# Exchanged weight halves by eight SP transfers instead of two GpSimd copies, and one warming product fewer

## The chip, the core and the metric

The kernel runs on one core of a Trainium2 chip. TensorE (PE) multiplies, VectorE (DVE), ScalarE (ACT) and GpSimd (POOL) work elementwise, and SyncE (SP) issues DMA transfers, as ACT and GpSimd can too. The metric is device time in microseconds; the time before is the median of 3 runs.

## The reference

A softmax over 7 taps per head (8 heads of 24 channels) weighs a causal convolution along the sequence; its result, 31232 tokens of 192 channels, goes through a multiplicative feed-forward layer:

```python
w = softmax(weight)                          # 8 x 7
out[b, s, h, g] = sum_k w[h, k] * x_pad[b, s + k, h, g]
x = out.reshape(31232, 192)
a = x @ w1                                   # 192 x 1024
b = x @ w2                                   # 192 x 1024
y = (a * b @ w3) @ w_out                     # 1024 x 1024, 1024 x 192
```

Inputs and output are float32; the kernel multiplies in bfloat16.

## The kernel before

**Work by rounds.** The tokens are cut into two halves (`NS = 2`) of 15616, and each half into rounds of `CH = 512` tokens. A round holds 512 tokens of both halves. `first_product(R)` runs over the 8 blocks of 128 features (`JT`, f = 0 to 7). For each it computes `pa` (w1) and `pb` (w2) on TensorE, ACT casts `pa` to `asb`, and VectorE multiplies `asb` by `pb` into `abT`. `second_product` multiplies `abT` by `W_sb`, the product of w3 and w_out made once on the chip near the start, and stores the output. Between the blocks of the first rounds, other steps are hung in by hand (`between`): convolutions, transposes, the products for `W_sb`.

**Why there are exchanged halves.** The 192 channels are cut into three parts of `Q = 64` (k = 0, 1, 2). An operand tile has 128 partitions: the 64 channels of one part for token half r = 0 in partitions 0 to 63, and for r = 1 in partitions 64 to 127. A product of L599 uses only the 64 partitions of its half, so the weights of each part have to stand in both partition halves. `wn[0]` holds w1's first 128 channels, `wn[1]` those of w2, `wn[2]` the remaining 64 of w1 (partitions 0 to 63) and of w2 (64 to 127). `wsw[k]`, in the profile `ws`, holds `wn[k]` with the two partition halves exchanged. `w_of` chooses between the two. For `pb` of each block the second and third product read `wsw[1]`: first its partitions 64 to 127, then 0 to 63.

**Order at the start.** The order on each engine is the order of the program (a manual schedule); semaphores are set by the framework. GpSimd issues the loads of the weights in two column ranges, 0 to 384 and 384 to 1024 (L227 to L233; the last of them is `wn[1]`, L231). The exchanged halves are made by `swap_w` (L222) with copies of 64 partitions: ACT and VectorE make columns 0 to 384, VectorE 256 to 640 of `ws[0]`, GpSimd the rest in the order in which the blocks come, with transfers for x (L158) and w3 (L677) between. Columns `W2 = 768` to 1024 serve blocks 6 and 7 and are GpSimd's last copies, in the order k = 0, 2, 1:

```python
load_w3(0, 4, range(2))
for k in (0, 2, 1):
    swap_w(k, W2, DFF, P)      # P: GpSimd's copy; two halves each
load_w3(0, 4, range(2, 4))
```

Meanwhile TensorE runs warming products on zeros (`warm`, L241) whose results nobody reads: 6 and 3, then 2, then 4 of 256 columns (L297) right after the product `bps` from which VectorE casts `Aband`, the band matrix of the convolution. Then come the first convolution (L331), its transposes (L419) and `first_product(0)`. SP has three loads at the start and its next instruction is the store of `convo` at 29.22 us.

Of the kernel before, what the change touches and what calls it, by code (L numbers as in the profile page):

```python
# [16 lines left out]
def kernel(  # L17
# [10 lines left out]
    nc = tc.nc  # L28
# [4 lines left out]
    DFF = moe_w1.shape[1]  # L33
# [10 lines left out]
    Q = 64  # L44
# [52 lines left out]
    def banks(name):  # L97
        return psum.tile([128, NS, CH], FP32, tag="banks", name=name)
# [23 lines left out]
    def group(r, e):  # L122
        return slice((2 * r + e) * C, (2 * r + e) * C + C)
# [57 lines left out]
    for r in range(NS):  # L181
        p = group(r, 0).start
# [12 lines left out]
        out=diag, in_=diag, pattern=[[-1, 128 + 8]], compare_op=ALU.is_equal,  # L195
# [13 lines left out]
    for i in range(4):  # L209
        d = diag[i * C:i * C + C, i * C + 2 * i:i * C + 2 * i + C]  # L210
        nc.vector.tensor_copy(
            out=cmask[i * C:i * C + C],
            in_=bass.AP(tensor=d.tensor, offset=d.offset, ap=[d.ap[0], [1, 2], [1, C]]))

    wn = [const.tile([128, DFF], BF16, name=f"wn{k}", tag=f"wn{k}") for k in range(3)]
    wsw = [const.tile([128, DFF], BF16, name=f"ws{k}", tag=f"ws{k}") for k in range(3)]

    W0, W1, W2 = 384, 640, 768

    def swap_w(k, lo, hi, f, halves=(1, 0)):  # L220
        for h in halves:
            f(out=wsw[k][Q * h:Q * h + Q, lo:hi], in_=wn[k][Q - Q * h:2 * Q - Q * h, lo:hi])  # L222
# [15 lines left out]
    def warm(n, wd=CH):  # L238
        t = banks("warm")
        for j in range(n):  # L240
            nc.tensor.matmul(  # L241
                t[:, j % 2, 0:wd].rearrange("p (a c) -> p a c", c=128), zeros,
                zeros.unsqueeze(1).to_broadcast([128, wd // 128, 128]), start=True, stop=True)
# [15 lines left out]
    for i in range(3):  # L259
# [3 lines left out]
        out=share[:, :, 0:K], in0=taps.unsqueeze(1).to_broadcast([H, H, K]), scalar=total,  # L263
        in1=diag[0:H, 0:H].unsqueeze(2).to_broadcast([H, H, K]), op0=ALU.mult, op1=ALU.mult)
    spread = banks("spread")
    for i in range(4):
# [6 lines left out]
        out=wsb, in_=spread[:, 0, 0:2 * H].rearrange("p (h k) -> p h k", h=H)  # L273
# [5 lines left out]
        out=cprod.rearrange("p h k (s two) -> p h k s two", two=2),  # L279
# [6 lines left out]
    p = group(1, 0).start  # L286
# [3 lines left out]
    for k in range(2):  # L290
# [3 lines left out]
            start=(k == 0), stop=(k == 1))  # L294
    nc.vector.tensor_copy(out=Aband,
                          in_=bps[:, 0, 0:C * H].rearrange("p (h s) -> p h s", s=C))
    warm(4, 256)  # L297


    xT = [const.tile([128, RING], BF16, name=f"xT{k}", tag=f"xT{k}") for k in range(NP)]  # L300
# [369 lines left out]
    def load_w3(j0, n, quarters=range(4)):  # L670
        if j0 not in w3b_of:
            t = stage.tile([128, 4 * n, GQ], BF16, tag=f"w3b{j0}", bufs=1, name="w3b")
            for j in range(j0, j0 + n, 2):
                w3b_of[j] = (t, 4 * (j - j0))
        t = w3b_of[j0][0]
        for i in quarters:
            nc.gpsimd.dma_start(  # L677
                out=t[C * i:C * i + C],
                in_=bass.AP(tensor=moe_w3.tensor, offset=j0 * 128 * DFF + i * GQ,
                            ap=[[DFF, C], [C * DFF, 4 * n], [1, GQ]]))  # L680
# [36 lines left out]
    for k in (0, 2, 1):  # L717
        swap_w(k, W1, W2, P)
    load_w3(0, 4, range(2))
    for k in (0, 2, 1):  # L720
        swap_w(k, W2, DFF, P)
    load_w3(0, 4, range(2, 4))

    trios = [tuple(range(R, R + TRIO)) for R in range(0, NR - 1, TRIO)]
# [12 lines left out]
    starts, chain, begun, room, p = {}, {}, set(), 0, -1  # L737
# [209 lines left out]
```

## Time and profile before

| | us |
|---|---|
| median of 3 runs | 511.01 (510.94 to 512.11) |
| the profiled execution | 511.07 |
| its span, first to last instruction | 509.3 |
| TensorE busy | 504.8 (99%) |
| VectorE busy | 446.6 (88%) |
| ACT busy | 347.3 (68%) |
| GpSimd busy | 229.5 (45%) |

Times in the trace are counted from the start of the span. PE stands for the products, PEld for TensorE's loads of weights, which overlap them; the ends of products are modelled. SPq is SP's queue of DMA issues, q0 the queue of GpSimd's transfers and q1 that of SP's. The bracket at the end of a row gives the engine's idle time before it and what released it. In the windows of the first 30 us the granted TensorE clock is given as 1.00 throughout; in the whole profile it is 0.999.

### The profile page before, as it was taken

To read this page: it belongs to the slowest core of one execution; us is meant where nothing else is said; L and a number is where in the kernel's file an instruction comes from. 1 tells how busy PE (TensorE), PEld (TensorE's weight loads), DVE (VectorE), ACT (ScalarE), POOL (GpSimd) and SP (SyncE) were. 2 spreads that over 40 slices of the span, in tenths; PEclk is the share of its full clock that TensorE was granted. 3 is DMA by queue.
4 is the path that set the end of the run, shared out by engine and by line. 5 is a ranking of instruction groups with operands and counts; after the bars stand their busy time and mean duration, and the time that the engine had idled before them with its cause. 6 is when DMAs were issued, how large, how long until landed. Compare 5 with 4: busy or idle time off the path is not lost.

```text
span 509.3 us, 13691 instructions
## 1 busy us (share of the span) xinstructions
PE 504.8 (99%) x5762; PEld 339.3 (67%) x5762; DVE 446.6 (88%) x403; ACT 347.3 (68%) x387; POOL 229.5 (45%) x303
## 2 busy tenths in 40 slices
PE   8999999999999999999999999999999999999997
PEld 4546865595569557855875596569557855965597
DVE  7898769999999899899989999999899999999930
ACT  6786667736778776477667767763776477457752
POOL 9965201333990597079509902970573067100000
PEclk9999999999999999999999999999999999999999
DMA  9999968999965999973979337986501500230025
GB/s 139 151 161 177 166 142 188 155 158 187 170 60 158 138 163 132 231 79 23 65 198 118 24 105 119 191 119 155 104 0 44 156 2 0 83 107 1 1 64 156
DMA packets 156825, 58.45 MB, mean 115 GB/s; under 512 B 112607, under 2 KB 156763, under 8 KB 156763
## 3 DMA queue, kind: packets, MB, share of 16 engines
q1 hardware_dynamic: 86043, 40.62, 37.2%
q0 software_dynamic: 70560, 16.85, 36.8%
q8 instruction: 45, 0.74, 0.6%
q14 instruction: 17, 0.14, 0.1%
q10 hardware_dynamic: 160, 0.10, 0.1%
HBM read 33.97 MB, written 34.85 MB: 135 GB/s over the span
## 4 chain that ended last, share of the span: by engine, by line
PE 99%; ACT 0%; DVE 0%; issue 0%
PE ops L624 32%; PE pa L599 31%; PE pb L599 31%; PE cps L331 1%; PE wps L696 1%; PE warm L241 1%; PE tps L404 0%; PE tps L419 0%; PE ops L649 0%; DVE abT L608 0%; PE cps L360 0%; ACT asb L606 0%; ACT convo L340 0%; PE bps L291 0%; ACT osb L653 0%
## 5 line engine op out<-in xcount | busy, mean ns | idle before, releaser
L608 DVE TENSOR_TENSOR abT<-asb,pb 128x1024 bf16<-128x1024 bf16 x240 | 292.7, 1221 | 30.4 <-ACT asb L606 14.5
L606 ACT CAST asb<-pa 128x1024 bf16<-128x1024 f32 x244 | 246.9, 1012 | 64.3 <-PE pa L599 64.0
L599 PEld LDWEIGHTS <-wn 64*128 64x128 bf16 x1488 | 138.6, 94 | 79.7 <-issue 1.6
L599 PEld LDWEIGHTS <-ws 64*128 64x128 bf16 x1488 | 129.7, 94 | 69.8 <-issue 1.7
L624 PE MATMUL ops<-W_sb,abT 128*128 128x192 bf16 x1936 | 163.7, 246 | 0.0
L624 PEld LDWEIGHTS <-abT 128*128 128x128 bf16 x1936 | 158.5, 98 | 6.4 <-issue 6.4
L599 PE MATMUL pb<-xT,wn 64*128 64x512 bf16 x408 | 111.2, 376 | 0.0
L599 PE MATMUL pa<-xT,wn 64*128 64x512 bf16 x408 | 110.1, 376 | 0.1
L599 PE MATMUL pa<-xT,ws 64*128 64x512 bf16 x408 | 110.2, 376 | 0.0
L599 PE MATMUL pb<-xT,ws 64*128 64x512 bf16 x408 | 108.5, 376 | 0.0
L629 ACT COPY osb<-ops 128x768 f32<-128x768 f32 (+1 forms) x61 | 48.4, 794 | 84.7 <-PE ops L624 82.9
L877 POOL COPY pace<-abT 1x2 bf16<-1x2 bf16 x57 | 10.9, 192 | 176.5 <-DVE abT L608 156.0
L599 PE MATMUL pb<-side,wn 64*128 64x512 bf16 (+1 forms) x336 | 88.8, 368 | 0.0
L599 PE MATMUL pa<-side,wn 64*128 64x512 bf16 (+1 forms) x336 | 87.3, 368 | 0.0
L599 PE MATMUL pa<-side,ws 64*128 64x512 bf16 (+1 forms) x336 | 87.3, 369 | 0.0
L515 DVE SCALAR_TENSOR_TENSOR acc<-raw,wC,acc 128x1024 f32<-128x1024 bf16 (+2 forms) x70 | 84.9, 1213 | 2.0
L599 PE MATMUL pb<-side,ws 64*128 64x512 bf16 (+1 forms) x336 | 85.8, 368 | 0.0
L542 POOL TENSOR_SCALAR tmp<-acc,wC 128x512 f32<-128x512 bf16 x42 | 65.7, 1565 | 1.2
L562 POOL TENSOR_TENSOR acc<-acc,tmp 128x512 f32<-128x512 f32 x35 | 44.3, 1267 | 2.9
L483 POOL DMA_DIRECT2D rows_c<-in_x_dram x50 | 37.1, 744 | 3.8 <-issue 2.8
L158 POOL DMA_DIRECT2D xb<-in_x_dram x50 | 32.3, 649 | 8.3 <-DMA xb<-in_x_dram 3.8
L515 DVE SCALAR_TENSOR_TENSOR acc<-side,wC,acc 128x1024 f32<-128x1024 bf16 (+1 forms) x20 | 24.3, 1217 | 3.7 <-DMA rows<-convo 3.2
(78 smaller groups left out, 189.5 us busy)
## 6 DMA issues: line engine op xcount, KB each, us to landing
out_dram<-osb SPq DMA_DIRECT2D x54, 384.0 KB
xb<-in_x_dram POOLq DMA_DIRECT2D x16, 240.0 KB, 7.2
out_dram<-osb SPq DMA_DIRECT2D x12, 192.0 KB
rows_c<-in_x_dram POOLq DMA_DIRECT2D x16, 130.0 KB, 4.3
rows_c<-in_x_dram POOLq DMA_DIRECT2D x12, 128.0 KB, 6.5
rows<-convo SPq DMA_DIRECT2D x6, 240.0 KB
xb<-in_x_dram POOLq DMA_DIRECT2D x6, 228.0 KB, 5.3
w3b<-in_moe_w_dram POOLq DMA_DIRECT2D x4, 256.0 KB, 4.8
```

What stands on the lines that cost most here:

```text
L158: nc.gpsimd.dma_start(out=tiles[js[0]][0][group(r, e), s:s + w, :], in_=bass.AP(tensor=x.tensor, offset=(r * TS + t - PAD) * D, ap=[[D, C] ...
L241: nc.tensor.matmul(t[:, j % 2, 0:wd].rearrange("p (a c) -> p a c", c=128), zeros, zeros.unsqueeze(1).to_broadcast([128, wd // 128, 128]), ...
L483: nc.gpsimd.dma_start(out=rows_c[lo:t1, k, r * Q:r * Q + Q], in_=x_rows[r * TS + lo:r * TS + t1, k * Q:k * Q + Q])
L515: nc.vector.scalar_tensor_tensor(out=side_of[p][:, k, o:o + t1 - t0] if last else a, in0=raw[:, HALO + lo - t0 - d:HALO + hi - t0 - d], sc ...
L542: nc.gpsimd.tensor_scalar(out=out, in0=pool_raw[0][:, HALO - d:HALO - d + CH], scalar1=wC[:, k, K - 1 - d:K - d], scalar2=None, op0=ALU.mult)
L562: nc.gpsimd.tensor_tensor(out=a, in0=a, in1=tmp[:, lo - t0:hi - t0], op=ALU.add)
L599: nc.tensor.matmul(p[:, r, f * N:f * N + N], w_of(i, k, r)[rs, ft * 128:(ft + 1) * 128], operand(R, k, rs), start=(k == 0), stop=(k == NP ...
L606: nc.scalar.copy(out=asb[:, :, 0:per * N], in_=pa[:, :, 0:per * N])
L608: nc.vector.tensor_tensor(out=ab[:, f0, :, 0:N], in0=asb[:, :, 0:N], in1=pb[:, :, 0:N], op=ALU.mult)
L624: nc.tensor.matmul(ops[:, g // 2, (g % 2) * D:(g % 2) * D + D], ab[:, jt, r, g * 128:(g + 1) * 128], W_sb[:, jt, :], start=(jt == 0), stop ...
L629: nc.scalar.copy(out=osb.rearrange("p (a g) d -> p a (g d)", g=2), in_=ops[:, 0:ng // 2, 0:2 * D])
L877: P(out=pace, in_=abT_of[R][0:1, ft, 1, 0:2])
```

## The change

`warm(4, 256)` becomes `warm(3, 256)`. For k = 1 and columns 768 to 1024, the two GpSimd copies of 64 partitions go, and SP issues eight transfers of 16 partitions by 256 columns (512 bytes a row, 8 KB each) from `wn[1]` to `wsw[1]`, SBUF to SBUF: the four for partitions 64 to 127 first. On SP they stand between the loads at the start and the store of `convo`; the first waits for the load of `wn[1]`. TensorE's two loads of these columns in block 6 wait for four transfers each, where they waited for a copy each. The order of everything else on every engine stays.

```diff
-    warm(4, 256)
+    warm(3, 256)
...
-    for k in (0, 2, 1):
+    for k in (0, 2):
         swap_w(k, W2, DFF, P)
+    for h in (1, 0):
+        for p in range(0, Q, 16):
+            nc.sync.dma_start(out=wsw[1][Q * h + p:Q * h + p + 16, W2:DFF],
+                              in_=wn[1][Q - Q * h + p:Q - Q * h + p + 16, W2:DFF])
     load_w3(0, 4, range(2, 4))
```

## The prediction

> **What bounds the kernel now.** I read the page first: busy shares and the chain that ended last. Then, for the first 20 us, where every edit lies, I read the chain in order of time, the timeline of each engine, and the waits.
>
> ```profile
> PE 504.8 (99%) x5762; PEld 339.3 (67%) x5762; DVE 446.6 (88%) x403; ACT 347.3 (68%) x387; POOL 229.5 (45%) x303
> PE 99%; ACT 0%; DVE 0%; issue 0%
> ```
>
> TensorE is busy for 504.8 of 509.3 us, and the chain of work that ended last is TensorE for 99%. So a change is worth what it takes off TensorE's own sequence, or what it makes TensorE wait. Here is the chain at the start (start, length, what):
>
> ```profile
> 1.06 3.06 PE warm L241 x9
> ...
> 5.64 0.85 PE warm L241 x4
> 6.49 0.38 PE cps L331 x14
> 6.87 0.02 issue
> 6.89 0.57 ACT convo L340
> 7.46 0.06 issue
> 7.52 0.90 PE tps L419 x10
> 8.42 0.11 issue
> 8.53 0.44 PE tps L419 x5
> 8.97 0.91 PE pa L599 x6
> 9.88 0.65 PE pb L599 x6
> ```
>
> The four warming products of L297 (their helper is L241) stand on the chain for 0.85 us, right ahead of the first convolution. From there the chain goes on without a break into the first product. This is the place of the first edit.
>
> **The warming product.** Four took 0.85 us, so one is 0.21 us, and that is the most that its removal can bring. What comes next must be ready too: the convolution reads Aband, which VectorE casts.
>
> ```profile
> 5.76 0.42 DVE L295 CAST Aband<-bps 128x256 bf16<-128x256 f32 x1
> 5.43 1.06 PE L241 MATMUL warm<-zeros 128*128 128x256 bf16 x4
> 6.42 0.33 PEld L331 LDWEIGHTS <-Aband 32*32 32x32 bf16 x26 [0.41 <-DVE Aband L295]
> ```
>
> Aband is ready at 5.76 + 0.42 = 6.18. A hand-over between engines takes about 0.06 us here (convo ends at 7.46 and tps starts at 7.52, above), so the weights could load at 6.24, and did at 6.42. On TensorE's side the convolution loaded 0.07 us before the modelled end of the last warming product (5.43 + 1.06 = 6.49); with three, that end is 6.28, and the load could come at 6.21. The later of 6.24 and 6.21 decides: **gain 0.18 us**, with the cast of Aband as the next thing late. The bounds are 0 (if something else held the load until 6.42) and 0.21.
>
> Does the 0.18 reach the end? The followers are released by TensorE or by each other (ACT waits 1.64 us for cps, and in the chain above tps follows ACT's convo):
>
> ```profile
> 6.89 0.89 ACT L340 CAST convo<-cps 128x480 bf16<-128x480 f32 x2 [1.64 <-PE cps L331]
> 7.42 0.84 POOL L222 COPY ws<-wn 64x256 bf16<-64x256 bf16 x2
> 8.21 2.75 POOL L158 DMA_DIRECT2D xb<-in_x_dram  x4
> ```
>
> GpSimd's first exchanged halves end at 7.42 + 0.84 = 8.26, and the first product would now start at about 8.79 instead of 8.97: still ready. So the 0.18 is carried to the first product, and from there TensorE is the chain.
>
> **The copies that leave GpSimd.** GpSimd loses two copies of about 0.4 us. They were the last of its six for columns 768 to 1024, and feature block 6 waited for them:
>
> ```profile
> 16.10 2.65 POOL L222 COPY ws<-wn 64x256 bf16<-64x256 bf16 x6
> 18.70 1.28 POOL L677 DMA_DIRECT2D w3b<-in_moe_w_dram  x2
> 18.54 0.38 PE L599 MATMUL pa<-xT,ws 64*128 64x512 bf16 x1
> 18.76 0.59 PE L599 MATMUL pb<-xT,ws 64*128 64x512 bf16 x2
> 18.80 0.09 PEld L599 LDWEIGHTS <-ws 64*128 64x128 bf16 x1 [0.16 <-POOL ws L222]
> ```
>
> The copies ended at 16.10 + 2.65 = 18.75, and the second exchanged half was loaded from 18.80 to 18.89, after a wait of 0.16 us. Its product began at 18.97 (18.76 + 0.59, less the 0.38 that one product takes). There was 0.08 us of slack. With everything 0.18 us earlier the old copies would have taken 0.1 us of the gain back; the transfers take that limit away and put their own in its place.
>
> The two w3b loads behind the copies start two copies sooner, at 18.70 - 2 x 2.65 / 6 = 17.8. I cost this lead at nothing, as VectorE first reads w3b at 29.30, after its other work:
>
> ```profile
> 29.30 1.24 DVE L685 STREAM_TRANSPOSE w3T<-w3b 128x1024 f32<-128x1024 f32 x1
> ```
>
> **The eight transfers.** SP gets a wait: the first transfer needs wn's second columns, whose load GpSimd issues at 6.78, the last of three in the window with these landings (min, median, max):
>
> ```profile
> 6.78 0.61 POOL L231 DMA_DIRECT2D wn<-in_moe_w_dram  x1
> DMA to landing us min/median/max: 4.2/4.3/4.4
> ```
>
> They land at 6.78 + 4.4 = 11.2, so SP issues from about 11.25. Behind SP's wait stands the store of convo at 29.22 (row below), and behind that the transposing loads that feed later rounds; they wait for convo, not for SP. No other queue is passed. The eight take unused completion semaphores or such as the loads at the start have long released, so none waits for another.
>
> TensorE's deadlines, moved by 0.18: the first four transfers (partitions 64 to 127) by 18.5, for the second pb product of block 6 (18.76 - 0.18, less 0.09 for the load); the last four by 18.97 - 0.18 - 0.09 = **18.7**.
>
> No small SBUF-to-SBUF transfer is in the trace, so I bound it by SP's small transfers beside GpSimd's loads:
>
> ```profile
> 29.22 0.74 SPq L395 DMA_DIRECT2D rows<-convo  x2
> 30.01 0.57 SPq L437 DMA_DIRECT2D taps_d<-taps  x1
> 33.60 6.07 SPq L442 DMA_DIRECT2D wC<-taps_d  x10
> 37.72 0.31 SPq L442 DMA_DIRECT2D wC<-taps_d  x1
> 38.84 0.29 SPq L442 DMA_DIRECT2D wC<-taps_d  x1
> SPq L442 <- DMA taps_d<-taps: 3.0, 1, 3.0
> SPq L442 <- DMA wC<-taps_d: 0.8, 1, 0.8
> ```
>
> *Fast end.* Two stores of 16 and 10 rows, the former the shape nearest to ours, went out in 0.74 us: a pitch of 0.39 with the gap. The taps_d store, issued at 30.01, had landed when the next instruction, which waits for it, began at 33.60: 3.6 us. So the eighth starts at 11.25 + 7 x 0.39 = 13.98 and lands at 17.6: 1.1 us of slack. *Slow end.* The ten wC loads are small and back to back. The eighth began at 37.72, which is 4.12 us after the first; the ninth waits for the landing of the first and began at 38.84, 5.24 us after it. The eighth of ours would start at 15.37 and land at 20.6, which is 1.9 us late. A cost below nothing is excluded: early data don't let TensorE start sooner than its own sequence.
>
> Which end? The queues of GpSimd's loads around the three places (share of 16 engines in 11 to 16, 29 to 33 and 33 to 38 us):
>
> ```profile
> q0 software_dynamic: 2121, 0.80, 141.3%
> q0 software_dynamic: 1231, 0.66, 128.0%
> q0 software_dynamic: 1284, 0.62, 99.9%
> ```
>
> Load alone doesn't order the two ends: the wC loads were slower under less of it. They read DRAM in pieces of 28 B, and ours, like the stores, read SBUF in rows of half a kilobyte and more. I go by the stores, moved up a little for the heavier load and the longer series: pitch 0.45, landing 4.2. The eighth lands at 11.25 + 3.15 + 4.2 = 18.6, just within 18.7; the fourth at 16.8, with room. **Stall 0**, with 0 to 1.9 us kept for the range.
>
> [...]
>
> The transfers also share the DMA engines. They move 64 KB; at 0.80 MB in 5 us that is 0.4 us of the queue. The nearest reader is the convolution inside block 4:
>
> ```profile
> 15.64 0.60 PE L360 MATMUL cps<-xb,Aband 32*32 32x120 bf16 x32
> DMA to landing us min/median/max: 5.5/6.4/7.3
> ```
>
> The second line is for the four xb loads issued from 8.21. The first lands at about 13.7 and is read at 15.64 - 0.18: over 1.7 us of slack against 0.4, so nothing.
>
> **The sum**, against the profiled execution of 511.07 us (span 509.3 and 1.8 us around it): -0.18 + 0 = 510.89. That execution is 0.06 above the median of 511.01, so the forecast for a median is 511.01 - 0.18 = **510.85** (510.83, rounded), a change of 0.04%. About 0.3%, or 1.5 us, is what a measurement of this kernel can tell from no change; its three runs alone span 1.2 us.
>
> **The rivals.**
>
> *Transfers somewhat late.* The last four land between 18.7 and 20.4, say 19.2. TensorE stands 0.5 us in block 6, net +0.3: 511.3. For it: my own landing is only 0.1 us ahead of the deadline. Against it: the stores.
>
> *Transfers far late: slower.* The same wait by the wC rows: landing 20.6, stall 1.9, net +1.7: 512.7, and more if the longer series slows further. It decides from a landing after 18.7 + 0.18 + 1.53 = 20.4 on. For it: eight in a row, as the wC loads. Against it: the slow end itself is only just past that point.
>
> *The clock.* The warming products keep TensorE busy until its rate doubles: one of 256 columns took 0.21 us before 6.49, while six of 512 columns over 64 rows (two halves side by side, so three passes) take 0.65, that is 0.22 for 512 columns, from 9.88 on. With less work ahead the doubling could come later. The warming lasted 5.4 us (1.06 to 6.49); a doubling later by as much would fall at 11.9, and the products from 8.8 on would lose half of that, 1.5 us: net +1.4, 512.4. Against it: the convolution moves up into the hole, so TensorE is idle for hardly 0.1 us. [...]
>
> *Nothing gained.* The load at 6.42 was held by something other than the warming products: 511.0.
>
> **How the numbers follow.** In time 0.50; somewhat late 0.33; far late 0.10; clock 0.04; nothing gained 0.03. Slower by over 0.3% is far late and half of the clock: 0.12. Faster by over 0.3% has no mechanism, as the most is 0.21 us; I leave 0.02 for the scatter of runs. Within: 0.86. The range reaches from 510.4, the likeliest case less 0.4 us of scatter, to 512.4, which takes in somewhat late and the clock and leaves out most of far late.
>
> **What would show it.** Right: in the profile after, three warming products and the convolution's load at about 6.24; SP's eight issues from 11.25 to about 14.8; the ws loads of block 6 at 18.4 to 18.8 with no wait put down to a DMA; GpSimd's second pair of w3b at about 17.8. Wrong: a gap on TensorE in front of block 6's pb products with a DMA of ws as releaser, or a first product that starts at 8.97 as before.

## The result: 0.6% slower, by a transfer that lands at 22.0 us

The changed kernel took 514.12 us (median of six runs, 513.10 to 515.51) against 511.04 us (510.92 to 512.11) for the kernel before, taken beside it. The ratio is 1.0059 with a 95% interval of 1.0038 to 1.0079. The forecast was 510.85 us with a range of 510.4 to 512.4, so it was wrong, and on the side that had been given 0.12. Five of the six runs of the changed kernel had a granted clock of 0.996 or 0.997, and one 1.0.

The profiled execution took 514.24 us with a span of 512.5, against 511.07 and 509.3. The page after, engine totals and the shares of the chain that ended last, then one group of part 5 (busy us, mean ns, idle before and its releaser):

```profile
PE 505.2 (99%) x5761; PEld 339.3 (66%) x5761; DVE 446.2 (87%) x403; ACT 347.3 (68%) x387; POOL 228.7 (45%) x301
PE 95%; DMA 2%; POOL 1%; SPq 1%; ACT 0%; DVE 0%; issue 0%; POOLq 0%
L599 PE MATMUL pb<-xT,ws 64*128 64x512 bf16 x408 | 109.1, 377 | 2.2 <-DMA ws<-wn 2.2
```

TensorE has one product fewer and is busy for almost the same time. New are 2% of the chain on DMAs and 1% each on SP's queue and GpSimd, and an idle time of 2.2 us in front of the pb products that read ws, ended by a DMA of ws. Here is the chain of the kernel after, from 6 to 24 us (start, length, what):

```profile
6.77 4.89 DMA wn<-in_moe_w_dram
11.66 0.02 issue
11.68 0.61 SPq L724
12.28 0.04 issue
12.32 0.58 SPq L724
...
15.50 0.59 SPq L724
16.08 0.04 issue
16.13 5.89 DMA ws<-wn
22.02 0.14 issue
22.16 0.61 PE pb L599 x4
```

In the kernel before, the chain from 7.52 us to the same products was TensorE and 0.11 us of issue. Now it is wn's load, eight issues on SP one behind the other, and the landing of the eighth. So what TensorE did before 22.02 doesn't set the time: whatever had gone better or worse there was waited away.

The timelines of the kernel after, PE, SP and POOL (start, busy time, what; in brackets the idle time before and its releaser):

```profile
6.24 0.88 PE L331 MATMUL cps<-xb,Aband 32*32 32x120 bf16 x64 [0.53 <-DVE Aband L295]
19.61 0.38 PE L599 MATMUL pb<-xT,ws 64*128 64x512 bf16 x1
22.16 0.37 PE L599 MATMUL pb<-xT,ws 64*128 64x512 bf16 x1 [2.18 <-DMA ws<-wn]
11.68 5.04 SPq L724 DMA_DIRECT2D ws<-wn  x8
16.09 1.76 POOL L222 COPY ws<-wn 64x256 bf16<-64x256 bf16 x4
17.80 1.28 POOL L677 DMA_DIRECT2D w3b<-in_moe_w_dram  x2
```

The second exchanged half's first product of block 6 began at 22.16; before, it began at 18.97. That is 3.19 us, and the span grew by 3.2. VectorE's abT of block 7 and of every later block stands 3.16 us later than before, so the whole loss is made here and nothing is added or given back in the 490 us behind it.

In this execution a second thing went wrong, and it is hidden by the wait. Stretches of the kernel after (window, length, busy us and count for PE, PEld, DVE, ACT, POOL, then the granted clock, the DMA share and GB/s):

```profile
3.98:7.40 3.42, 2.44 (x78) 1.35 (x77) 2.23 (x7) 2.02 (x4) 3.40 (x7) 1.00 1.40 177
7.40:10.80 3.40, 3.40 (x25) 2.22 (x27) 2.64 (x8) 2.17 (x6) 3.32 (x6) 0.50 1.04 152
10.80:14.00 3.20, 3.20 (x32) 1.39 (x30) 2.11 (x2) 2.43 (x3) 2.75 (x9) 1.00 1.36 147
```

By the trace's record of the clock it was full from 3.98 us on, fell back to half from 7.40 to 10.81, and was full again. Blocks 1 to 5 therefore ended 0.86 us later than before, where the same start at a full clock put them 0.26 us earlier (the run with two transfers, below). Without the fall TensorE would, as an estimate from these two, have arrived 1.1 us sooner and waited 1.1 us longer for the same landing.

### The profile page after: what moved, and what is told of

It is laid out like the page before. It is cut to its first block, busy times and chain, and to the rows that moved or that the text cites. A ratio compares the mean times of both kernels' runs of the same rounds, so it can differ in the third digit from the quotient of the medians.

```text
span 512.5 us, 13701 instructions
## 1 busy us (share of the span) xinstructions
PE 505.2 (99%) x5761; PEld 339.3 (66%) x5761; DVE 446.2 (87%) x403; ACT 347.3 (68%) x387; POOL 228.7 (45%) x301
## 4 chain that ended last, share of the span: by engine, by line
PE 95%; DMA 2%; POOL 1%; SPq 1%; ACT 0%; DVE 0%; issue 0%; POOLq 0%
PE ops L624 32%; PE pa L599 30%; PE pb L599 30%; PE cps L331 1%; DMA ws<-wn 1%; PE wps L696 1%; DMA wn<-in_moe_w_dram 1%; SPq L724 1%; PE tps L404 0%; POOL xb L158 0%; PE ops L649 0%; DVE abT L608 0%; POOL wn L227 0%; POOL wn L228 0%; ACT asb L606 0%
```

## The experiments

Two theories stood at the start. *Landing*: the whole loss is the eighth transfer's issue and landing; of these, either the slow pitch of SP or the slow landing beside GpSimd's loads could be the cause. *Clock*: the missing warming product costs a stretch at half the clock. The kernel before, beside them, took 511.09 us (23 runs) with the single warming product, the first series of the transfers alone, the two transfers and the quiet probe, and 511.07 us (25 runs) with the others.

**One warming product fewer, nothing else.**

```diff
-    warm(4, 256)
+    warm(3, 256)
```

> The kernel before with one warming product fewer; GpSimd's two copies stay. Theory 1 (the loss is the late landing of the eight transfers, and the clock's fall only hides behind it): no transfers, so no 3 us; TensorE waits about 0.1 us for the last copy in block 6, and the time is 510.9 to 511.2, plus at most 1 us in runs in which the clock is halved for a window. Theory 2 (the missing warming product lets the clock fall back from 7.4 to 10.8 us, and that is the loss): 512 to 514, with a granted clock of 0.997 in most runs.

Measured: 511.09 us (510.86 to 513.20, 12 runs), ratio 0.9996 [0.9980, 1.0013]. The granted clock was 0.999 or 1.0 in all twelve. In the trace of this kernel (PE, POOL and weight loads):

```profile
6.22 0.77 PE L331 MATMUL cps<-xb,Aband 32*32 32x120 bf16 x64 [0.50 <-DVE Aband L295]
16.11 2.65 POOL L222 COPY ws<-wn 64x256 bf16<-64x256 bf16 x6
18.81 0.09 PEld L599 LDWEIGHTS <-ws 64*128 64x128 bf16 x1 [0.36 <-POOL ws L222]
```

The convolution starts at 6.22, held by Aband, and blocks 1 to 5 end 0.33 us sooner than in the trace of the kernel before. Then GpSimd's sixth copy, which ends when it always did, takes 0.14 us back in block 6, and from about 60 us on the shift is +0.08.

The 0.33 us can't be put down to the product, though. Here is the same place in a kernel with four warming products (the second trace of the next experiment):

```profile
5.24 0.60 PE L241 MATMUL warm<-zeros 128*128 128x256 bf16 x4
6.23 0.77 PE L331 MATMUL cps<-xb,Aband 32*32 32x120 bf16 x64 [0.39 <-DVE Aband L295]
```

Its convolution also starts at 6.23, held by Aband, and its blocks 1 to 5 also end 0.33 us sooner. In the trace of the kernel before the four products took 1.06 us, here 0.60. The difference is the clock at the start: the first record of a full clock lies at 6.88 us in the trace of the kernel before, at 4.25 here and at 5.02 in the trace with three products above. (The windows print 1.00 also ahead of the first record, so they don't show it.) With the clock up at 4.25 us, four products were done before Aband was ready, and taking one away gains nothing; with the clock up at 6.88 us, in the trace of the kernel before, the fourth stands in the way. No trace has three products and a late clock, so its worth there, forecast as 0.18 us, wasn't measured. At the end the product is worth nothing that the times show, and in these twelve runs it has no clock price.

**The eight transfers, with four warming products.** The diff is the change without its first hunk, so `warm(4, 256)` stays. There are two traces of it.

> The changed kernel with the fourth warming product back: the eight transfers alone. Theory 1: the same time as the changed kernel, 513.5 to 514.5, as the landing of the eighth at about 22.0 us sets the end of block 6 whatever went before; TensorE waits over 2.5 us for it, more than the 2.2 of the changed kernel where the clock stays up. Theory 2: back at about 511, clock 0.999.

Measured: 514.87 us (512.92 to 514.99, 6 runs), ratio 1.0068 [1.0043, 1.0094]. The transfers alone make the whole loss. The chain of this kernel in its first trace:

```profile
15.97 4.78 DMA ws<-wn
20.74 0.14 issue
20.88 0.61 PE pb L599 x4
```

The eighth lands at 20.74, TensorE waits 1.94 us, and the end is 1.87 us later. That profiled execution took 512.92, though, and the five others 514.73 to 514.99 with a granted clock of 0.997 instead of 1.0. So something of about 2 us was missing from the trace.

> The kernel with the transfers alone (four warming products) again, for a second profile: five of its six runs had a granted clock of 0.997 and took 514.7 to 515.0, the profiled one 1.0 and 512.92. If TensorE's stand of 2 us in block 6 lets its clock be halved for one window afterwards, a profile of a run of 514.8 shows a stretch of about 3.4 us at clock 0.50 that begins between 19 and 24 us, and block 7 takes twice as long in it. If the clock is lost at the start, as in the changed kernel's profile, the stretch lies before 12 us and the time is about 513.

The run of the second trace took 514.86 us at a clock of 0.996, and shows it. Its PE timeline:

```profile
21.16 0.46 PE L599 MATMUL pb<-xT,ws 64*128 64x512 bf16 x1 [2.28 <-DMA ws<-wn]
```

and the stretches around the stand, with columns as above:

```profile
18.80:21.30 2.50, 0.22 (x4) 0.14 (x4) 0.63 (x3) 0.85 (x1) 2.42 (x5) 1.00 1.42 190
21.30:24.70 3.40, 3.40 (x25) 1.94 (x23) 1.46 (x2) 0.59 (x1) 2.52 (x5) 0.50 1.40 162
24.70:28.00 3.30, 3.30 (x34) 1.48 (x32) 2.33 (x4) 2.36 (x3) 1.33 (x3) 1.00 1.60 191
```

TensorE stood for 2.28 us, and from 21.32 to 24.73 it got half the clock. The products behind the stand began 0.28 us later than in the first trace (21.16 against 20.88), yet from block 7 on the shift against before is +3.72 us against +1.88: the stand's echo costs about 1.56 us. Whether the long runs of the kernel after, 515.43 and 515.51, had the same echo isn't shown. Their clock of 0.996 and 0.997 allows it, but runs of 513.10 and 513.25 had the same clock, and the one trace of this kernel has its fall at 7.40 and none behind the stand.

**Two transfers of 64 partitions instead of eight of 16.**

```diff
-        for p in range(0, Q, 16):
-            nc.sync.dma_start(out=wsw[1][Q * h + p:Q * h + p + 16, W2:DFF],
-                              in_=wn[1][Q - Q * h + p:Q - Q * h + p + 16, W2:DFF])
+        nc.sync.dma_start(out=wsw[1][Q * h:Q * h + Q, W2:DFF],
+                          in_=wn[1][Q - Q * h:2 * Q - Q * h, W2:DFF])
```

> The changed kernel with one transfer of 64 partitions for each half instead of four of 16: the same bytes and rows in two issues. Theory 1 in the form that the issue of eight costs (pitch 0.63 us, 4.45 us from first to eighth): the second starts at 12.3 us, lands 4.5 to 5.9 us later at 16.8 to 18.2, in time for 18.7, and the kernel takes 510.8 to 511.1 (up to 1 us more where the clock falls). Rival (the rows wait in the DMA engines behind GpSimd's loads, however they are issued): landing at about 22, 514.

Measured: 511.17 us (511.08 to 511.45, 12 runs), ratio 0.9995 [0.9982, 1.0009]. SP and PE in this kernel:

```profile
11.49 1.18 SPq L723 DMA_DIRECT2D ws<-wn  x2
18.50 0.59 PE L599 MATMUL pb<-xT,ws 64*128 64x512 bf16 x2
18.72 0.38 PE L599 MATMUL pb<-xT,wn 64*128 64x512 bf16 x1
```

Two issues took 0.54 and 0.60 us, each for four times the bytes. They landed 6.2 and 5.8 us after their issue, at 17.71 and 17.91: as slow in flight as the eight, but issued in time, and block 6 has no wait. It ran 0.26 us sooner than before; 0.13 us of that was still there at 50 us and 0.14 at 506 us, and then the last stores ended 0.21 us later than before.

**Four transfers of 32 partitions.** The same loop as in the change, in steps of 32.

> The changed kernel with four transfers of 32 partitions instead of eight of 16. By the issue pitch of 0.63 us the fourth starts at 11.55 + 1.9 = 13.4, and with a landing of 4.9 us after the issue (what the fourth of eight took) it lands at 18.3, in time for 18.7: 510.9 to 511.3. If the landing goes on growing with the number in flight, 19 to 20 and 511.3 to 512.5.

Measured: 511.23 us (510.94 to 512.63, 10 runs), ratio 0.9999 [0.9986, 1.0012].

```profile
11.77 3.15 SPq L724 DMA_DIRECT2D ws<-wn  x4
18.71 0.84 PE L599 MATMUL pb<-xT,ws 64*128 64x512 bf16 x2
19.19 0.39 PE L599 MATMUL pb<-xT,wn 64*128 64x512 bf16 x1
```

Starts were 11.77, 12.43, 13.70 and 14.33 (the second issue took 1.22), and landings 5.97, 5.68, 4.74 and 4.72 us later: the last at 19.05. TensorE lost a quarter of a microsecond in block 6 (the shift goes from -0.05 to +0.19). So four are just too late, two are not, and eight are far too late.

**The pitch by itself.** The kernel before with eight such transfers near 360 us into a tile that nothing else uses; GpSimd reads from it after the fourth and the eighth. Here no load of GpSimd is in flight.

```diff
+    probe = const.tile([128, 256], BF16, name="probe")
+    seen = const.tile([128, 2], BF16, name="seen")
...
         turn(p)
+        if p == 6:
+            for h in (1, 0):
+                for q in range(0, Q, 16):
+                    nc.sync.dma_start(out=probe[Q * h + q:Q * h + q + 16, :],
+                                      in_=wn[1][Q - Q * h + q:Q - Q * h + q + 16, W2:DFF])
+            for h in (1, 0):
+                P(out=seen[Q * h:Q * h + Q, :], in_=probe[Q * h:Q * h + Q, 0:2])
```

> The kernel before with eight more transfers of the same form (16 partitions, 256 columns, SBUF to SBUF, to a tile that nobody else reads), issued by SP at the end of the seventh stage near 390 us, where GpSimd's queue is empty; two small GpSimd copies read them, so the wait for the landing shows. If the pitch of 0.63 us and the landing of 4.5 to 5.9 us belong to the form, they are seen again. If they come from GpSimd's loads in the same DMA engines, the pitch is 0.35 to 0.4 and the landing 2 to 2.5 us after the issue. The time of the kernel stays at 511.

Measured: 510.93 us (one run). SP's and POOL's timelines:

```profile
360.50 5.03 SPq L921 DMA_DIRECT2D probe<-wn  x8
366.81 0.18 POOL L924 COPY seen<-probe 64x2 bf16<-64x2 bf16 x1 [2.18 <-DMA probe<-wn]
```

Eight issues in 5.03 us, as in the change: the pitch of 0.63 belongs to this form of transfer, not to the load. What in the form sets it (the direction, the length of a row) was not varied. The landing does belong to the load: 1.71 to 1.79 us after the issue here, where the same transfers took 4.5 to 5.9 near 12 us.

**The eight with less load beside them.** The change, with the load of the third block of x and the first pair of w3b moved behind GpSimd's last copies.

```diff
     load_x(1)
-    load_x(2)
...
-    load_w3(0, 4, range(2))
     for k in (0, 2):
         swap_w(k, W2, DFF, P)
+    load_x(2)
+    load_w3(0, 4, range(2))
```

> The changed kernel with GpSimd's loads of x for the third block and of the first half of w3 moved behind its last copies, so that from about 15 us on the DMA engines have little else to do while the eight transfers run (their issue still takes 4.45 us from first to eighth). If the landing of 4.3 to 5.9 us comes from GpSimd's loads in front of the transfers in the DMA engines: the first still land late, the eighth, issued at about 16.0, lands about 2 to 3 us later at 18 to 19, TensorE waits 0 to 0.3 us, and the kernel takes 510.9 to 511.3. If it comes from the eight transfers themselves: landing at 21 to 22, 513 to 515.

Measured: 516.46 us (513.39 to 517.23, 6 runs), ratio 1.0080 [1.0053, 1.0106]. For the disputed transfers it gives the answer, and elsewhere it pays for it. The DMA queues between 11 and 16 us (packets, MB, share of 16 engines), in the kernel after:

```profile
q0 software_dynamic: 2069, 0.78, 141.2%
q1 hardware_dynamic: 41, 0.01, 1.1%
```

and in this kernel, the same queues, then a line of its PE timeline, then one of its waits (us in total, times, longest):

```profile
q0 software_dynamic: 1191, 0.45, 80.3%
q1 hardware_dynamic: 160, 0.04, 3.8%
```

```profile
18.48 0.59 PE L599 MATMUL pb<-xT,ws 64*128 64x512 bf16 x2
```

```profile
PE cps L331 <- DMA xb<-in_x_dram: 2.6, 2, 1.8
```

In the kernel after, SP's queue (q1) moved 41 packets in these 5 us; with GpSimd's queue (q0) at 80% instead of 141% it moved 160. From issue to landing, in us, at the same pitch:

| transfer | 1 | 2 | 3 | 4 | 5 | 6 | 7 | 8 |
|---|---|---|---|---|---|---|---|---|
| kernel after | 5.91 | 5.88 | 5.43 | 4.98 | 4.52 | 4.80 | 4.77 | 5.89 |
| less load | 3.79 | 3.32 | 2.88 | 2.43 | 1.97 | 1.78 | 1.78 | 1.77 |

The eighth landed at 17.98, before its deadline, and the timeline shows block 6 without a wait, 0.28 us sooner than before. But GpSimd's loads behind come later too, and they are missed: the product for W_sb that starts at 47.27 us has waited 1.4 us for VectorE, whose transposing of w3b waits for its load; near 60 us the convolution waits 2.6 us for xb in two pieces; and a stretch at half the clock follows at 63.2. The shift is +6.15 from 77 us on.

**No transfers: GpSimd's six copies moved ahead of the first w3b pair.** With three warming products.

```diff
-    load_w3(0, 4, range(2))
     for k in (0, 2, 1):
         swap_w(k, W2, DFF, P)
-    load_w3(0, 4, range(2, 4))
+    load_w3(0, 4, range(4))
```

> No transfers: the kernel before with three warming products, and GpSimd's last six copies moved ahead of its first two loads of w3. The copies end at about 17.5 us, so block 6 has no wait at all. By the shift seen with three warming products (0.2 to 0.33 us sooner in block 6) and the loss of up to 0.3 us at other places later, 510.7 to 511.1: the same as before within what can be measured. Rival (the later w3 loads make VectorE's transposing wait at 29 us): 511.5 or more.

Measured: 513.82 us (512.52 to 515.59, 12 runs), ratio 1.0046 [1.0030, 1.0063], a miss: I had expected no change or a gain. A line of the waits of this kernel, and three of its chain:

```profile
PE cps L331 <- DMA xb<-in_x_dram: 1.8, 1, 1.8
```

```profile
42.84 8.03 DMA xb<-in_x_dram
...
51.15 8.89 DMA xb<-in_x_dram
60.09 0.39 PE cps L331 x21
```

Block 6 is fine (+0.04). The first w3b pair now starts at 17.51 instead of 14.78; the loads that GpSimd issues from about 31 us on come 2.5 us later, the last x load lands at 60 us, and TensorE waits 1.8 us for it: +2.46 from 77 us on. GpSimd's load queue has next to no slack up to there, in this direction.

## Why the prediction was wrong

**The step that failed is the term "eight transfers", put at a stall of 0.** It measured 3.2 us: the products behind the landing began 3.19 us later than before. Its three factors were all low. The first issue came at 11.68 instead of 11.25, as wn landed 4.89 us after its issue and not 4.4. The pitch was 0.636 instead of 0.45, which is 1.30 us over seven steps; the eighth went out at 16.13, where I had 14.40. The landing took 5.89 instead of 4.2. Together 0.43 + 1.30 + 1.69 = 3.42 us, from 18.60 to 22.02. By these figures the pitch or the landing alone would have missed 18.7.

**The choice between the ends was wrong, and the ends were too close.** I chose the stores of convo as "the shape nearest to ours", for a pitch of 0.39. They go from SBUF to DRAM; the runs show 0.54 to 0.64 us per issue for SBUF to SBUF, with or without load and for 16 to 64 partitions, but for one of 1.22. The wC rows, with 4.12 us from the first to the eighth, were nearly right (4.45), though they load from DRAM. For the landing no row of the trace was from the right place: all came from times with GpSimd's queue at 100 to 128%, while at 11 to 16 us it was at 141%. I had quoted that share and set the load aside, as it doesn't order the two ends; the run with less load shows that it sets the landing of these transfers. Why the wC rows were slower than the stores under less load stays open. Even my slow end, 20.6, was lower than the three landings of these eight that were traced at this place (20.74, 21.02 and 22.02).

**The rival "far late" was the right mechanism,** with the right point of decision: 22.02 is past 20.4. Its price of +1.7 was too small, for the reason above and for another that no rival held: the stand of TensorE (2.28 us) was itself followed by a stretch at half the clock (21.32 to 24.73 us), about 1.56 us more in the second trace of the transfers alone.

**Right were** the deadline of 18.7 (landings at 17.91 and 17.98 cost nothing, one at 19.05 a quarter of a microsecond); the w3b pair at 17.80 and its lead worth nothing; and the convolution at 6.24 held by Aband.

**The term "warming product" came out by luck.** The convolution did start 0.18 us sooner, but in the second trace of the transfers alone, with all four products and the clock up at 4.25 us, it starts at 6.23 as well. The sum took the products at 0.21 us each, from a trace with a late clock; in the trace of after the three ended at 5.71 and not at 6.28. Nor was the 0.18 "carried to the first product, and from there" on: without a stall the two traces with three products end at +0.07 and -0.14 us near 490 us, which the times don't show.

**The clock rival fell.** In 24 runs of the two kernels with three warming products and no stall the clock was 0.999 or more, and neither lost time. The kernel before, with four, had 0.996 or 0.997 in three of its 48 runs. The fall at 7.40 in the profiled execution of after isn't forced by the missing product: the run with the copies first has the same start, a raise at 3.96 and 2.42 us of products in the stretch behind it (after: 3.98 and 2.44), and kept its clock there. What told these two apart stays open.

## What to carry to other kernels

Before a copy is turned into transfers, take a row of the same form and the load of the queues at that very place; here the trace had no such row, the slow end (a landing at 20.6 us) came nearer than the fast one (17.6), and even it was too fast (20.74, 21.02 and 22.02 were measured). The last landing was what cost, and two larger transfers beat eight small ones: the two went out in 1.18 us and the eight in 5.03, for the same bytes, and the kernel took 511.17 us with two and 514.12 with eight. Beside the busy queue a transfer that feeds a tight deadline needed more room (4.5 to 6.2 us to the landing instead of 1.75), and moving that queue's work out of the way cost more later than the wait (a shift of 6.15 us from 77 us on, against 3.2). And when a small shift is read from two traces, look first whether the clock came up at the same time in both (here at 6.88 us in one and at 4.25 in another).

## What the runs showed of the hardware that was not expected

- An issue on SP of an SBUF-to-SBUF transfer took 0.54 to 0.64 us (pitch 0.63 in the series of eight), quiet or loaded, for 8 KB as for 32 KB; one of 16 KB took 1.22.
- Its landing is about 1.75 us after the issue in quiet and 4.5 to 6.2 us beside GpSimd's loads, 1.8 to 3.8 us where these were lighter.
- A stand of TensorE of 2.28 us was followed by half the clock (second trace of the transfers alone: no product from 18.88 to 21.16, clock 0.50 from 21.32 to 24.73). Stands of 1.94 us (the first trace) and 2.18 us (the kernel after) were not. Near 60 us the run with less load stood for 2.6 us in two pieces, the longer of 1.8, and got half the clock from 63.2 on; the run with the copies first stood for 1.8 us and kept its clock. The fall at 7.40 in the kernel after came behind a stretch (3.98 to 7.40) with only 0.98 us without a product. The two stretches at half the clock that the traces of the kernel after and of the transfers alone show were 3.41 us long (7.40 to 10.81 and 21.32 to 24.73). What decides whether the clock falls isn't shown, and no run was made to test it.
